# Attention followed by a two-layer feed-forward block: q and k of batches 1 to 7 turned by crossbar DMA instead of TensorE, and another way to set up the bias band

## The chip, the cores and the metric

The kernel runs on one NeuronCore of a Trainium2 chip. Its engines work side by side, each through its own queue of instructions: TensorE (PE: matmuls, and its weight loads, PEld), VectorE (DVE), ScalarE (ACT), GpSimd (POOL) and SyncE (SP). Transfers are issued from the queues of SP and POOL and carried out by 16 shared DMA engines. The metric is the device time of one execution in microseconds (us). The runs of the kernel before took 419.15 us in the median (418.38 to 419.69).

## The reference

Inputs are q, k and v of 8 batches, 8 heads, 576 tokens and 64 numbers a head, a bias table of 32 buckets by 8 heads, and the two weight matrices (512 x 2048 and 2048 x 512). All are float32.

```
scores = scale * q @ k^T                      # 576 x 576 for each batch and head
bias   = bias_table[bucket(|i - j|)]          # depends only on |i - j|; from 128 on one bucket
attn   = exp(scores + bias - max) ; attn /= sum(attn)
x      = (attn @ v), heads side by side       # 4608 x 512
h      = x @ w_in ; g = max(0.01 h, h) ; out = g @ w_out
```

The output is 4608 x 512, float32.

## The kernel before

**Items.** The work on attention goes over 32 pairs of heads: item n is batch n // 4 and pair n % 4. The loop at line 410 runs over n, and each round does the scores and exps of pair n, the product with V of pair n - 1, and the transposition of q and k of pair n + 1. In the gaps it places pieces of the feed-forward block (`moe(1)`, lines 428 to 457), four matmuls of 512 columns each, at most eight in a round, alternately of the first and of the second layer. A tile of 512 tokens of the first layer can start once the batches that it needs are finished, so there is none before round 4 ends. What is left is done at the end (`moe_rest`).

**q and k.** GpSimd loads them by cast DMA (`load_qk`, L106) in bfloat16, 96 partitions with six consecutive tokens each. `pair_rows` (L219) copies the two heads of a pair side by side on VectorE. `transpose_q` and `transpose_k` (L227, L238) turn six blocks of 96 x 128 on TensorE into a PSUM tile of the pool `ps_m`, which has three buffers and also serves the feed-forward block; then VectorE copies them to SBUF and puts the tokens in their order (L234, L245). The last 64 keys of each head are copied once more behind the others (L249).

**Scores to output.** `qk_mm` (L252) makes scores with keys on the partitions, in six parts a pair (L259, L265, L268, L269); ScalarE takes the exp (L279 to L286); `band` (L294) multiplies the parts near the diagonal by exp(bias - bias of the last bucket), which is 1 further away. `av` (L310) multiplies with V and a column of ones, and VectorE divides (L326, L327). `x_transposes` (L330) turns the result for the feed-forward block. Its output goes out by SP (L364) from a pool of four buffers.

**The bias band.** The exponentials of the table, 8 heads on 8 partitions, are spread on VectorE into a row of 512 numbers a head (L147 to L165). SP writes the rows (8 KB) to DRAM and reads them back in two transfers to `hk`, each partition one element further than the last (L166 to L173). This gives the band mirrored, and `make_band` (L175) turns it round into `eb`, with a copy for the last 64 keys in `eb4`: pair 0 on VectorE, pairs 1 to 3 on GpSimd. In round 0 the band products of pair 0 are put off to the end of the round (L287 to L292), so that VectorE prepares pair 1 before.

**Order.** The program gives the order on every engine in the order of its lines: L68 lists PE, ACT, DVE, POOL and SP. On GpSimd the loads for batch 1, the weights and V of batch 1 (L415 to L419) therefore stand behind the three `make_band` calls. Later batches are loaded in round p = 1 of the batch before (L420). VectorE's buffer memsets (L187 to L195) stand behind the work on the bias rows.

Of the kernel before, what the change touches and what calls it, by code (L numbers as in the profile page):

```python
# [10 lines left out]
FP32 = mybir.dt.float32  # L11
BF16 = mybir.dt.bfloat16

AF = mybir.ActivationFunctionType
ALU = mybir.AluOpType
# [22 lines left out]
def kernel(  # L38
# [26 lines left out]
    n_cc = DM // P  # L65
    BAND = 128

    ctx.enter_context(tc.manual_schedule(engines={ET.PE, ET.Activation, ET.DVE, ET.Pool, ET.SP}))  # L68

    per = ctx.enter_context(tc.tile_pool(name="per", bufs=1))  # L70
    qt_pool = ctx.enter_context(tc.tile_pool(name="qt", bufs=2))
    pr_pool = ctx.enter_context(tc.tile_pool(name="pr", bufs=4))
    op_pool = ctx.enter_context(tc.tile_pool(name="op", bufs=2))
    rc_pool = ctx.enter_context(tc.tile_pool(name="rc", bufs=4))
    gt_pool = ctx.enter_context(tc.tile_pool(name="gt", bufs=2))
# [3 lines left out]
    ps_m_pool = ctx.enter_context(tc.tile_pool(name="ps_m", bufs=3, space=bass.MemoryType.PSUM))  # L79

    ident = per.tile([P, P], BF16, name="ident")
    warm = per.tile([P, 1], FP32, name="warm")
    nc.vector.memset(warm, 0.0)
    nc.scalar.activation(warm, warm, AF.Exp)

    xT = [per.tile([P, NT], BF16, name=f"xT{p}") for p in range(n_pairs)]
    w_in_sb = per.tile([P, n_cc, DF], BF16, name="w_in_sb")
# [44 lines left out]
                in_=v[b, h0 + e : h1 : 2, NJ * P : S, :].rearrange("h s d -> s h d"),  # L132
            )

    tabT = per.tile([H, NB], FP32, name="tabT")
    with nc.allow_non_contiguous_dma(reason="a table of 256 numbers"):
        nc.sync.dma_start(out=tabT, in_=bias_table.rearrange("u h -> h u"))
    load_qk(0, 0, 2)
    make_identity(nc, ident)

    e8 = per.tile([H, NB], BF16, name="e8")
    UW = 4 * P
    BW = 3 * P
    ub = per.tile([H, UW], BF16, name="ub")
    nc.vector.memset(ub, 1.0)  # L147
    negc = per.tile([H, 1], FP32, name="negc")
    nc.vector.tensor_scalar(negc, tabT[:, NB - 1 : NB], -1.0, None, op0=ALU.mult)
    nc.scalar.activation(e8, tabT, AF.Exp, bias=negc[:, 0:1], scale=1.0)  # L150
    C0 = 2 * P - 1
    small = NB // 2
    nc.vector.tensor_copy(out=ub[:, C0 : C0 + small], in_=e8[:, 0:small])
    for u, lo, hi in bucket_runs(NB, BAND, S):
        if lo >= small:
            nc.vector.tensor_copy(
                out=ub[:, C0 + lo : C0 + hi + 1],
                in_=e8[:, u : u + 1].to_broadcast([H, hi - lo + 1]),
            )
    row = ub[:, :]  # L160
    nc.vector.tensor_copy(
        out=ub[:, C0 - BAND + 1 : C0],
        in_=bass.AP(tensor=row.tensor, offset=row.offset + C0 + BAND - 1,
                    ap=[list(row.ap[0]), [-1, BAND - 1]]),
    )  # L165
    udr = nc.dram_tensor("u_row", [H, UW], BF16, kind="Internal")  # L166
    hk = per.tile([P, H, BW], BF16, name="hk")
    nc.sync.dma_start(out=udr.ap(), in_=ub)
    for h0, h1 in ((0, 2), (2, H)):
        nc.sync.dma_start(  # L170
            out=hk[:, h0:h1, :],
            in_=bass.AP(tensor=udr, offset=h0 * UW, ap=[[1, P], [UW, h1 - h0], [1, BW]]),
        )  # L173

    def make_band(eng, p):  # L175
        t = hk[:, 2 * p : 2 * p + 2, :]
        eng.tensor_copy(
            out=eb[:, 2 * p : 2 * p + 2, :],
            in_=bass.AP(tensor=t.tensor, offset=t.offset + BW - 1,
                        ap=[list(t.ap[0]), [BW, 2], [-1, BW]]),  # L180
        )
        for e in range(2):
            r = slice(e * SL, (e + 1) * SL)
            eng.tensor_copy(out=eb4[r, p, :], in_=eb[r, 2 * p + e, e * SL : e * SL + P + SL])

    load_qk(0, 2, H)
    for i in range(NBUF):  # L187
        nc.vector.memset(v4[i], 0.0)
        for e in range(2):
# [2 lines left out]
    for i in range(2):  # L192
        nc.vector.memset(kts_[i][:, S : S + P], 0.0)
        nc.vector.memset(at_[i][:, ATW : ATW + SL], 1.0)
        nc.vector.memset(at4_[i][:, S : S + SL], 1.0)  # L195
    load_v(0, 0, 2, True)
    load_v(0, 2, H, False)
    for j in range(1, n_pairs):
        make_band(nc.gpsimd, j)

    def load_w_in(half):
        o = slice(half * (DF // 2), (half + 1) * (DF // 2))
        for c in range(n_cc):
            nc.gpsimd.dma_start(out=w_in_sb[:, c, o], in_=moe_w_in[c * P : (c + 1) * P, o])

    def load_w_out():
        for g in range(n_fc // 4):
            nc.gpsimd.dma_start(
                out=w_out_sb[:, 4 * g : 4 * g + 4, :],
                in_=moe_w_out[g * 512 : (g + 1) * 512, :].rearrange("(f p) e -> p f e", p=P),  # L210
            )
# [2 lines left out]
    items = [(b, p) for b in range(B) for p in range(n_pairs)]  # L214
    qts, kts, ops_ = {}, {}, {}

    prs = {}

    def pair_rows(n, which):  # L219
        src = {"q": qn, "k": kn}[which]  # L220
        b, p = items[n]
        t = pr_pool.tile([RQ, NC, 2 * D], BF16, name="pr")
        nc.vector.tensor_copy(out=t.rearrange("r c (e d) -> r c e d", e=2),  # L223
                              in_=src[b % NBUF][0:RQ, 2 * p : 2 * p + 2, :, :].rearrange("r e c d -> r c e d"))
        prs[n, which] = t

    def transpose_q(n):  # L227
        qs = prs.pop((n, "q"))
        ps = ps_m_pool.tile([P, 8 * P], BF16, name="ps_tq", tag="m")
        for c in range(NC):  # L230
            nc.tensor.transpose(ps[:, c * RQ : (c + 1) * RQ], in_=qs[0:RQ, c, :],  # L231
                                identity=ident[0:RQ, 0:RQ])
        qt = qt_pool.tile([P, S], BF16, name="qt")
        nc.vector.tensor_copy(out=qt.rearrange("p (r c) -> p r c", c=NC),  # L234
                              in_=ps[:, 0:S].rearrange("p (c r) -> p r c", c=NC))
        qts[n] = qt

    def transpose_k(n):  # L238
        ks = prs.pop((n, "k"))
        ps = ps_m_pool.tile([P, 8 * P], BF16, name="ps_tk", tag="m")  # L240
        for c in range(NC):
            nc.tensor.transpose(ps[:, c * RQ : (c + 1) * RQ], in_=ks[0:RQ, c, :],  # L242
                                identity=ident[0:RQ, 0:RQ])
        kt = kts_[n % 2]
        nc.vector.tensor_copy(out=kt[:, 0:S].rearrange("p (r c) -> p r c", c=NC),  # L245
                              in_=ps[:, 0:S].rearrange("p (c r) -> p r c", c=NC))
        for e in range(2):
            r = slice(e * D, (e + 1) * D)
            nc.vector.tensor_copy(out=kt[r, S + e * SL : S + (e + 1) * SL], in_=kt[r, NJ * P : S])  # L249
        kts[n] = kt  # L250

    def qk_mm(n, u):  # L252

# [21 lines left out]
    def exp_band(n, u, ps):  # L275
        b, p = items[n]
        at, at4 = at_view(n), at4_[n % 2]
        if u < NJ:
            nc.scalar.activation(at[:, :, u, 0:512], ps, AF.Exp, scale=scale)  # L279
        elif u == NJ:  # L280
            nc.scalar.activation(  # L281
                at[:, :, :, 512:S],
                ps[:, :, 0 : NJ * SL].rearrange("p e (c i) -> p e c i", i=SL),
                AF.Exp, scale=scale)
        else:
            nc.scalar.activation(at4[:, 0:S], ps.rearrange("p e i -> p (e i)")[:, 0:S], AF.Exp, scale=scale)  # L286
        if n > 0:  # L287
            band(n, u)
        elif u == NJ + 1:
            make_band(nc.vector, 0)  # L290
            for j in range(NJ + 2):
                band(n, j)  # L292

    def band(n, u):  # L294
        b, p = items[n]
# [106 lines left out]
            while made["ready"] < n_tt and (made["ready"] + 1) * TT <= (b + 1) * S:  # L402
                made["ready"] += 1

    pair_rows(0, "q")
    pair_rows(0, "k")
    transpose_q(0)
    transpose_k(0)
    N = len(items)
    for n in range(N + 1):  # L410
        live = n < N
        if live:
            b, p = items[n]
            if n == 0:
                load_qk(1, 0, H)  # L415
                load_w_in(0)
                load_w_in(1)
                load_v(1, 0, H, False)
                load_w_out()  # L419
            elif p == 1 and 0 < b < B - 1:  # L420
                load_qk(b + 1, 0, H)
                load_v(b + 1, 0, H, False)
            if n + 1 < N:
                pair_rows(n + 1, "q")
                pair_rows(n + 1, "k")
            ps_a, ps_b = qk_mm(n, 0), qk_mm(n, 1)
            exp_band(n, 0, ps_a)
        moe(1)
        if live:
            exp_band(n, 1, ps_b)  # L430
        if n > 0:
            av(n - 1, 0)
        if n + 1 < N:
            transpose_q(n + 1)
        moe(1)
        if live:
            ps_a, ps_b = qk_mm(n, 2), qk_mm(n, 3)
            exp_band(n, 2, ps_a)
        moe(1)
        if live:  # L440
            exp_band(n, 3, ps_b)
        if n > 0:
            av(n - 1, 1)
        if n + 1 < N:
            transpose_k(n + 1)
        moe(1)
        if live:
            ps_a, ps_b = qk_mm(n, 4), qk_mm(n, 5)
            exp_band(n, 4, ps_a)
        moe(1)  # L450
        if n > 0:
            x_transposes(n - 1)
            finished(n - 1)
        moe(1)
        if live:
            exp_band(n, 5, ps_b)
        moe(2)
# [31 lines left out]
```

The softmax here doesn't subtract the row's maximum and nothing guards it: scores larger than these inputs give would overflow.

## Time and profile before

| | us |
|---|---|
| median of the runs | 419.15 |
| the profiled execution | 419.69 |
| its span, from first to last instruction | 417.9 |
| TensorE busy in the span | 394.9 |
| ScalarE busy | 247.0 |
| VectorE busy | 226.7 |
| GpSimd busy | 67.9 |

A line of the stages gives a stretch of the span, then for each engine its busy time and the number of its instructions, the granted clock of TensorE, the share of the DMA engines and what they moved. A line of the chain of waits gives the start, the length and what the time went to: an engine's work on a tile with its line, or a transfer. A line of the groups gives line, engine, operation, tile, shapes and count, then busy time and the mean of one in ns, then the idle time before it and what ended it. PEld lines are weight loads, which overlap matmuls. "issue" is time in which nothing that the profile shows was waited for. Numbers behind a tile's name tell buffers apart.

### The profile page before, as it was taken

Reading aid. Unit: us, or ns where it says so; the run is one execution under the profiler, and the core shown is the slowest. Engines: PE = TensorE matmul, PEld = TensorE weight load, DVE = VectorE, ACT = ScalarE, POOL = GpSimd, SP = SyncE. Lnnn points to the kernel's source line nnn. Section 1 sums busy time; section 2 is a strip of 40 time slices with the busy share of each in tenths; the row PEclk is TensorE's granted clock in tenths of the full one; section 3 lists DMA queues with packets and bytes.
Section 4 is the critical chain, followed back from the end, with each engine's and each line's share of the span. In section 5 each row is a group of like instructions: output and inputs, shape, how many; then the busy total and the mean of one; then the engine's idle time right before and its main releaser. Section 6 shows DMA issues by size and latency. Waiting matters only on the chain.

```text
span 417.9 us, 9069 instructions
## 1 busy us (share of the span) xinstructions
PE 394.9 (94%) x3872; PEld 203.8 (49%) x3872; DVE 226.7 (54%) x585; ACT 247.0 (59%) x339; POOL 67.9 (16%) x97
## 2 busy tenths in 40 slices
PE   1897699999999999999999999999999999999996
PEld 1365365455555555445554455555555454444442
DVE  6789667765666655655566666655666431010111
ACT  1768477866666676666666666667666633333310
POOL 8474631301022100410041004000000000000000
PEclk9999999999999999999999999999999999999999
DMA  8969999458027710944091706300000001010112
GB/s 115 131 99 202 183 204 166 36 33 140 27 37 71 123 44 27 83 75 91 25 83 30 137 27 39 46 25 27 27 27 27 27 27 50 25 52 25 52 50 76
DMA packets 60096, 29.16 MB, mean 70 GB/s; under 512 B 39056, under 2 KB 54424, under 8 KB 60056
## 3 DMA queue, kind: packets, MB, share of 16 engines
q0 software_dynamic: 53536, 18.36, 40.5%
q1 hardware_dynamic: 6520, 10.24, 6.8%
q8 instruction: 30, 0.49, 0.5%
q14 instruction: 10, 0.08, 0.1%
HBM read 37.49 MB, written 9.45 MB: 112 GB/s over the span
## 4 chain that ended last, share of the span: by engine, by line
PE 82%; DMA 8%; ACT 3%; POOL 2%; DVE 2%; issue 1%; SPq 0%
PE ps_o L321 7%; PE ps_s L259 6%; DMA w_in_sb<-in_moe_w_in_dram 3%; DMA vn_104<-in_v_dram 2%; PE ps_s L268 2%; PE ps_o L323 2%; DMA hk<-u_row 2%; PE ps_tx L335 2%; PE ps_tq L231 1%; PE ps_tk L242 1%; PE ps_s L265 1%; ACT at_109 L279 1%; DMA u_row<-ub 1%; PE pm_5795 L358 1%; PE pm_4291 L358 1%; PE pm_4115 L358 1%
## 5 line engine op out<-in xcount | busy, mean ns | idle before, releaser
L347 PEld LDWEIGHTS <-w_in_sb 128*128 128x128 bf16 x576 | 50.0, 98 | 73.3 <-issue 22.6
L279 ACT ACTIVATE at_109<-ps_s 128x1024 bf16<-128x1024 f32 x64 | 64.4, 1021 | 22.7 <-PE ps_s L259 22.6
L358 PEld LDWEIGHTS <-gt 128*128 128x128 bf16 x576 | 52.5, 98 | 51.4 <-issue 0.4
L279 ACT ACTIVATE at_110<-ps_s 128x1024 bf16<-128x1024 f32 x64 | 64.8, 1021 | 20.1 <-PE ps_s L259 20.1
L308 DVE TENSOR_TENSOR at_110<-at_110,eb 128x512 bf16<-128x512 bf16 (+1 forms) x64 | 32.5, 510 | 44.4 <-ACT at_110 L279 39.7
L308 DVE TENSOR_TENSOR at_109<-at_109,eb 128x512 bf16<-128x512 bf16 (+1 forms) x64 | 32.0, 505 | 39.0 <-ACT at_109 L279 36.6
L321 PEld LDWEIGHTS <-at_109 128*128 128x128 bf16 x640 | 29.3, 101 | 13.2 <-DVE opair L327 3.9
L327 DVE TENSOR_TENSOR opair<-ps_o,rcp 128x320 bf16<-128x320 f32 x64 | 31.5, 491 | 2.2
L321 PEld LDWEIGHTS <-at_110 128*128 128x128 bf16 x640 | 27.8, 99 | 10.0 <-DVE opair L327 3.0
L125 POOL DMA_DIRECT2D vn_104<-in_v_dram x16 | 14.2, 898 | 70.0 <-PE ps_o L323 39.9
L234 DVE COPY qt<-ps_tq 128x576 bf16<-128x576 bf16 x32 | 23.9, 747 | 0.5 <-PE ps_tq L231 0.5
L259 PE MATMUL ps_s<-qt,kt_107 64*128 64x512 bf16 x128 | 21.4, 403 | 2.1 <-DVE kt_107 L245 1.2
L125 POOL DMA_DIRECT2D vn_103<-in_v_dram x16 | 13.9, 881 | 55.5 <-PE ps_o L323 53.0
L231 PE MATMUL ps_tq<-ident,pr 96*128 96x96 bf16 x192 | 14.2, 213 | 7.9 <-DVE pr L223 7.8
L259 PE MATMUL ps_s<-qt,kt_108 64*128 64x512 bf16 x128 | 20.9, 398 | 0.7 <-ACT at_110 L279 0.3
L326 DVE RECIPROCAL rcp<-ps_o 128x5 f32<-128x5 f32 x64 | 12.2, 190 | 14.6 <-PE ps_o L323 14.6
L321 PE MATMUL ps_o<-vn_103,at_109 128*128 128x65 bf16 x320 | 16.1, 200 | 2.4 <-DVE opair L327 2.1
L321 PE MATMUL ps_o<-vn_104,at_109 128*128 128x65 bf16 x320 | 15.4, 197 | 2.2 <-DMA vn_104<-in_v_dram 2.2
L323 PEld LDWEIGHTS <-at_0_111 128*128 128x128 bf16 x160 | 16.1, 100 | 1.1 <-issue 0.8
L321 PE MATMUL ps_o<-vn_103,at_110 128*128 128x65 bf16 x320 | 15.1, 197 | 1.5 <-DVE opair L327 1.5
L281 ACT ACTIVATE at_110<-ps_s 128x512 bf16<-128x512 f32 x16 | 9.6, 598 | 10.9 <-PE ps_s L265 10.9
L323 PEld LDWEIGHTS <-at_1_112 128*128 128x128 bf16 x160 | 15.8, 98 | 0.2 <-DVE at_1_112 L308 0.2
(873 smaller groups left out, 814.7 us busy)
## 6 DMA issues: line engine op xcount, KB each, us to landing
out_dram<-y SPq DMA_DIRECT2D x36, 256.0 KB, 2.0
qn_100<-in_q_dram POOLq DMA_DIRECT2D x4, 576.0 KB, 6.1
kn_102<-in_k_dram POOLq DMA_DIRECT2D x4, 576.0 KB, 8.2
w_in_sb<-in_moe_w_in_dram POOLq DMA_DIRECT2D x8, 256.0 KB, 11.6
vn_104<-in_v_dram POOLq DMA_DIRECT2D x16, 128.0 KB, 4.9
w_out_sb<-in_moe_w_out_dram POOLq DMA_DIRECT2D x4, 512.0 KB, 10.0
qn_99<-in_q_dram POOLq DMA_DIRECT2D x3, 576.0 KB, 6.1
kn_101<-in_k_dram POOLq DMA_DIRECT2D x3, 576.0 KB, 9.4
```

Source lines behind the costliest of these rows:

```text
L125: nc.gpsimd.dma_start(out=vn[i][:, c, h0:h1, 0:D], in_=v[b, h0:h1, c * P : (c + 1) * P, :].rearrange("h s d -> s h d"),)
L231: nc.tensor.transpose(ps[:, c * RQ : (c + 1) * RQ], in_=qs[0:RQ, c, :], identity=ident[0:RQ, 0:RQ])
L234: nc.vector.tensor_copy(out=qt.rearrange("p (r c) -> p r c", c=NC), in_=ps[:, 0:S].rearrange("p (c r) -> p r c", c=NC))
L259: nc.tensor.matmul(ps[:, e, :], lhsT=kt[r, u * P : (u + 1) * P], rhs=qt[r, 0:512], start=True, stop=True)
L279: nc.scalar.activation(at[:, :, u, 0:512], ps, AF.Exp, scale=scale)
L308: nc.vector.tensor_tensor(out=o, in0=o, in1=m, op=ALU.mult)
L321: nc.tensor.matmul(ps[:, ic, :], lhsT=at[:, o : o + P], rhs=vn[i][:, c, 2 * p + e, :], start=(c == 0), stop=False)
L323: nc.tensor.matmul(ps[:, ic, :], lhsT=at4[:, ic * P : (ic + 1) * P], rhs=v4[i][:, p, e, :], start=False, stop=True)
L326: nc.vector.reciprocal(rcp, ps[:, :, D : D + 1])
L327: nc.vector.tensor_tensor(out=opair[:, :, e * D : (e + 1) * D], in0=ps[:, :, 0:D], in1=rcp.to_broadcast([P, NJ + 1, D]), op=ALU.mult)
L347: nc.tensor.matmul(pm, lhsT=w_in_sb[:, c, f * P : (f + 1) * P], rhs=xT[c][:, t0 : t0 + TT], start=(c == 0), stop=(c == n_cc - 1))
L358: nc.tensor.matmul(pm, lhsT=gt[:, f, ts * P : (ts + 1) * P], rhs=w_out_sb[:, f, :], start=(f == 0), stop=(f == n_fc - 1))
```

## The change

The change has four parts.

1. q and k of batches 1 to 7 are no longer turned by TensorE. `pair_rows` copies q and k of a pair into one tile of 96 x 1536, in round n for pair n + 2, and SP issues one crossbar transpose of it into a tile of 128 x 12 x 96 in SBUF (`turn_by_dma`). `transpose_q` and `transpose_k` stand where they stood; for these batches they hold only VectorE's copy to token order, now out of SBUF. Batch 0 is turned by TensorE as before. The pools of the two tiles have three buffers each.
2. The bias rows are made on all 128 partitions, from a table read to all of them, and written to DRAM 128 times (1 MB). The band is read back unmirrored, straight into `eb` and `eb4`, by four transfers. `make_band` and the put-off of pair 0's band products are gone, and so is ScalarE's first activation on an empty column.
3. The buffer memsets now stand ahead of the work on the rows. GpSimd's loads of batch 0 stand ahead of it too; q and k of later batches are loaded one round earlier (p = 0). The first-layer weights come in four transfers instead of eight, and all weights ahead of V of batch 1.
4. The order on POOL and SP is no longer fixed by the program's lines; the scheduler of the framework sets it.

```diff
-    ctx.enter_context(tc.manual_schedule(engines={ET.PE, ET.Activation, ET.DVE, ET.Pool, ET.SP}))
+    ctx.enter_context(tc.manual_schedule(engines={ET.PE, ET.Activation, ET.DVE}))
...
-    pr_pool = ctx.enter_context(tc.tile_pool(name="pr", bufs=4))
+    pr_pool = ctx.enter_context(tc.tile_pool(name="pr", bufs=3))
+    tu_pool = ctx.enter_context(tc.tile_pool(name="tu", bufs=3))
...
-    warm = per.tile([P, 1], FP32, name="warm")
-    nc.vector.memset(warm, 0.0)
-    nc.scalar.activation(warm, warm, AF.Exp)
+    make_identity(nc, ident)
...
-    ub = per.tile([H, UW], BF16, name="ub")
-    nc.vector.memset(ub, 1.0)
...
-    nc.sync.dma_start(out=udr.ap(), in_=ub)
-    for h0, h1 in ((0, 2), (2, H)):
-        nc.sync.dma_start(
-            out=hk[:, h0:h1, :],
-            in_=bass.AP(tensor=udr, offset=h0 * UW, ap=[[1, P], [UW, h1 - h0], [1, BW]]),
-        )
-
-    def make_band(eng, p):
...
     for i in range(NBUF):
         nc.vector.memset(v4[i], 0.0)
...
+    load_qk(0, 0, 2)
     load_v(0, 0, 2, True)
+    load_qk(0, 2, H)
     load_v(0, 2, H, False)
-    for j in range(1, n_pairs):
-        make_band(nc.gpsimd, j)
...
+    tab = per.tile([P, NB, H], FP32, name="tab")
+    nc.sync.dma_start(
+        out=tab.rearrange("p u h -> p (u h)"),
+        in_=bass.AP(tensor=bias_table.tensor, offset=bias_table.offset, ap=[[0, P], [1, NB * H]]),
+    )
+    UW = 4 * P
+    ub = per.tile([P, H, UW], BF16, name="ub")
+    nc.vector.memset(ub, 1.0)
+    nc.vector.tensor_tensor(out=tab, in0=tab, in1=tab[:, NB - 1 : NB, :].to_broadcast([P, NB, H]), op=ALU.subtract)
+    e8 = per.tile([P, H, NB], BF16, name="e8")
+    nc.scalar.activation(e8, tab.rearrange("p u h -> p h u"), AF.Exp)
...
+    urows = nc.dram_tensor("u_rows", [P, H, UW], BF16, kind="Internal")
+    for h0, h1 in ((0, 2), (2, H)):
+        nc.sync.dma_start(out=urows.ap()[:, h0:h1, :], in_=ub[:, h0:h1, :])
+    for h0, h1 in ((0, 2), (2, H)):
+        nc.sync.dma_start(
+            out=eb[:, h0:h1, :],
+            in_=bass.AP(tensor=urows, offset=h0 * UW + P - 1, ap=[[H * UW - 1, P], [UW, h1 - h0], [1, 3 * P]]),
+        )
+    for e in range(2):
+        nc.sync.dma_start(
+            out=eb4[e * SL : (e + 1) * SL, :, :],
+            in_=bass.AP(tensor=urows, offset=e * UW + P - 1, ap=[[H * UW - 1, SL], [2 * UW, n_pairs], [1, P + SL]]),
+        )
...
+    def pair_rows(n):
+
+        b, p = items[n]
+        t = prs[n] = pr_pool.tile([RQ, 2, NC, 2 * D], BF16, name="pr")
+        for j, src in enumerate((qn, kn)):
+            nc.vector.tensor_copy(out=t[:, j, :, :].rearrange("r c (e d) -> r c e d", e=2),
+                                  in_=src[b % NBUF][0:RQ, 2 * p : 2 * p + 2, :, :].rearrange("r e c d -> r c e d"))
+
+    def by_dma(n):
+        return items[n][0] > 0
+
+    def turn_by_dma(n):
+        t = turned[n] = tu_pool.tile([P, 2 * NC, RQ], BF16, name="tu")
+        nc.sync.dma_start_transpose(out=t, in_=prs.pop(n).rearrange("r j c d -> r (j c d)"))
+
+    def turned_pair(n, j):
+
+        if by_dma(n):
+            return turned[n][:, j * NC : (j + 1) * NC, :].rearrange("p c r -> p r c")
+        ps = ps_m_pool.tile([P, 8 * P], BF16, name="ps_t", tag="m")
+        for c in range(NC):
+            nc.tensor.transpose(ps[:, c * RQ : (c + 1) * RQ], in_=prs[n][0:RQ, j, c, :],
+                                identity=ident[0:RQ, 0:RQ])
+        return ps[:, 0:S].rearrange("p (c r) -> p r c", c=NC)
+
     def transpose_q(n):
...
+        qt = qts[n] = qt_pool.tile([P, S], BF16, name="qt")
+        nc.vector.tensor_copy(out=qt.rearrange("p (r c) -> p r c", c=NC), in_=turned_pair(n, 0))
...
-        if n > 0:
-            band(n, u)
-        elif u == NJ + 1:
-            make_band(nc.vector, 0)
-            for j in range(NJ + 2):
-                band(n, j)
+        band(n, u)
...
                 load_qk(1, 0, H)
-                load_w_in(0)
-                load_w_in(1)
+                load_weights()
                 load_v(1, 0, H, False)
-                load_w_out()
+            elif p == 0 and 0 < b < B - 1:
+                load_qk(b + 1, 0, H)
             elif p == 1 and 0 < b < B - 1:
-                load_qk(b + 1, 0, H)
                 load_v(b + 1, 0, H, False)
...
+            if n + 1 < N and not by_dma(n + 1):
+                pair_rows(n + 1)
+            if n + 2 < N and by_dma(n + 2):
+                pair_rows(n + 2)
+                turn_by_dma(n + 2)
```

More of the change, by code (lines that the diff above doesn't have):

```diff
@@ L133, in load_v @@
             )
[L135 to L145, printed above, removed]
-    ub = per.tile([H, UW], BF16, name="ub")
-    nc.vector.memset(ub, 1.0)
[L148 to L158, printed above, removed]
-            )
[L160 to L167, printed above, removed]
-    nc.sync.dma_start(out=udr.ap(), in_=ub)
-    for h0, h1 in ((0, 2), (2, H)):
-        nc.sync.dma_start(
-            out=hk[:, h0:h1, :],
-            in_=bass.AP(tensor=udr, offset=h0 * UW, ap=[[1, P], [UW, h1 - h0], [1, BW]]),
-        )
-    def make_band(eng, p):
[L176 to L186, printed above, removed]
     for i in range(NBUF):
@@ L195 @@
         nc.vector.memset(at4_[i][:, S : S + SL], 1.0)
+    load_qk(0, 0, 2)
     load_v(0, 0, 2, True)
+    load_qk(0, 2, H)
     load_v(0, 2, H, False)
-    for j in range(1, n_pairs):
-        make_band(nc.gpsimd, j)
-    def load_w_in(half):
-        o = slice(half * (DF // 2), (half + 1) * (DF // 2))
+    tab = per.tile([P, NB, H], FP32, name="tab")
[3 more added lines that the diff above has]
+    )
@@ new lines @@
+    UW = 4 * P
[4 more added lines that the diff above has]
+    nc.scalar.activation(e8, tab.rearrange("p u h -> p h u"), AF.Exp)
+    C0 = 2 * P - 1
+    small = NB // 2
+    nc.vector.tensor_copy(out=ub[:, :, C0 : C0 + small], in_=e8[:, :, 0:small])
+    for u, lo, hi in bucket_runs(NB, BAND, S):
+        if lo >= small:
+            nc.vector.tensor_copy(
+                out=ub[:, :, C0 + lo : C0 + hi + 1],
+                in_=e8[:, :, u : u + 1].to_broadcast([P, H, hi - lo + 1]),
+            )
@@ new lines @@
+    row = ub[:, :, :]
+    nc.vector.tensor_copy(
+        out=ub[:, :, C0 - BAND + 1 : C0],
+        in_=bass.AP(tensor=row.tensor, offset=row.offset + C0 + BAND - 1,
+                    ap=[list(row.ap[0]), [UW, H], [-1, BAND - 1]]),
+    )
[6 more added lines that the diff above has]
+            in_=bass.AP(tensor=urows, offset=h0 * UW + P - 1, ap=[[H * UW - 1, P], [UW, h1 - h0], [1, 3 * P]]),
+        )
@@ L203, in load_w_in, with load_weights @@
+    for e in range(2):
+        nc.sync.dma_start(
+            out=eb4[e * SL : (e + 1) * SL, :, :],
+            in_=bass.AP(tensor=urows, offset=e * UW + P - 1, ap=[[H * UW - 1, SL], [2 * UW, n_pairs], [1, P + SL]]),
+        )
+    def load_weights():
         for c in range(n_cc):
-            nc.gpsimd.dma_start(out=w_in_sb[:, c, o], in_=moe_w_in[c * P : (c + 1) * P, o])
-    def load_w_out():
+            nc.gpsimd.dma_start(out=w_in_sb[:, c, :], in_=moe_w_in[c * P : (c + 1) * P, :])
         for g in range(n_fc // 4):
@@ L215 @@
     qts, kts, ops_ = {}, {}, {}
-    prs = {}
-    def pair_rows(n, which):
-        src = {"q": qn, "k": kn}[which]
+    prs, turned = {}, {}
+    def pair_rows(n):
         b, p = items[n]
[L222 to L225, printed above, removed]
-    def transpose_q(n):
[L228 to L236, printed above, removed]
@@ L238, in transpose_k @@
-    def transpose_k(n):
[L239 to L246, printed above, removed]
+        t = prs[n] = pr_pool.tile([RQ, 2, NC, 2 * D], BF16, name="pr")
@@ L247, in transpose_k @@
+    def transpose_q(n):
+        qt = qts[n] = qt_pool.tile([P, S], BF16, name="qt")
+        nc.vector.tensor_copy(out=qt.rearrange("p (r c) -> p r c", c=NC), in_=turned_pair(n, 0))
+    def transpose_k(n):
+        kt = kts[n] = kts_[n % 2]
+        nc.vector.tensor_copy(out=kt[:, 0:S].rearrange("p (r c) -> p r c", c=NC), in_=turned_pair(n, 1))
         for e in range(2):
@@ L249, in transpose_k @@
             nc.vector.tensor_copy(out=kt[r, S + e * SL : S + (e + 1) * SL], in_=kt[r, NJ * P : S])
-        kts[n] = kt
     def qk_mm(n, u):
@@ L403, in finished @@
                 made["ready"] += 1
-    pair_rows(0, "q")
-    pair_rows(0, "k")
+    pair_rows(0)
     transpose_q(0)
@@ L415 @@
                 load_qk(1, 0, H)
-                load_w_in(0)
-                load_w_in(1)
+                load_weights()
                 load_v(1, 0, H, False)
-                load_w_out()
+            elif p == 0 and 0 < b < B - 1:
+                load_qk(b + 1, 0, H)
             elif p == 1 and 0 < b < B - 1:
-                load_qk(b + 1, 0, H)
                 load_v(b + 1, 0, H, False)
-            if n + 1 < N:
-                pair_rows(n + 1, "q")
-                pair_rows(n + 1, "k")
+            if n + 1 < N and not by_dma(n + 1):
[3 more added lines that the diff above has]
+                turn_by_dma(n + 2)
             ps_a, ps_b = qk_mm(n, 0), qk_mm(n, 1)
```

## The prediction

> **What bounds the kernel now.** I read the whole-span rows first, then busy time by stage, then the chain of work in two stretches, then the rows of what the change touches. The page, engines and slices:
>
> ```profile
> PE 394.9 (94%) x3872; PEld 203.8 (49%) x3872; DVE 226.7 (54%) x585; ACT 247.0 (59%) x339; POOL 67.9 (16%) x97
> ...
> PE   1897699999999999999999999999999999999996
> ```
>
> Busy time by stage (span of the stage, then busy us and instructions of each engine):
>
> ```profile
> 30.00:40.00 10.00, 8.05 (x129) 4.98 (x129) 9.19 (x26) 8.13 (x11) 4.39 (x6) 1.00 1.16 202
> 40.00:50.00 10.00, 5.84 (x84) 3.42 (x85) 6.46 (x17) 5.80 (x8) 5.03 (x8) 1.00 1.72 182
> ...
> 160.00:200.00 40.00, 40.00 (x433) 20.64 (x432) 24.46 (x61) 26.90 (x37) 6.31 (x8) 1.00 0.51 72
> ```
>
> There are two regimes. From about 80 us PE never rests, while VectorE is 61% and ScalarE 67% busy; before that PE has gaps. The chain in the steady stage is PE work end to end, and the transposes of q and k are links of it:
>
> ```profile
> 163.52 0.26 PE ps_tq L231 x6
> 163.78 0.86 PE pm_2584 L358 x4
> ...
> 166.92 0.26 PE ps_tk L242 x6
> 167.18 0.86 PE pm_2584 L358 x4
> ```
>
> The first score matmuls (L259) of two pairs stand at 161.19 and 172.28, so a pair takes 11.09 us, of which 0.26 + 0.26 = 0.52 us is these transposes. Each matmul row shows 0.2 us (14.2 us for a line in the union), but they are pipelined, and the chain's 0.26 us for six is what PE pays. In the first 50 us the chain is made of transfers:
>
> ```profile
> 4.99 4.93 DMA u_row<-ub
> 9.93 0.40 SPq L170
> 10.34 0.04 issue
> 10.38 7.68 DMA hk<-u_row
> 18.05 0.05 issue
> 18.11 1.08 POOL eb L177
> ...
> 26.11 11.04 DMA w_in_sb<-in_moe_w_in_dram
> ...
> 39.45 9.69 DMA vn_104<-in_v_dram
> ```
>
> So GpSimd makes bands until 24 us, the loads queued behind them start there, and V of batch 1 lands at 49.1. Score matmuls begin at 10.0, 15.1, 24.4, 30.7, 37.2, 45.2, 57.0, 65.5, 74.0 and 83.6 us for pairs 0 to 9, and at 327.5 for the last.
>
> **What the Trainium skill says.** "DMA: Bandwidth & Descriptors", section "DMA Transpose (X-bar)": the plain crossbar transpose can only be issued by Sync or ScalarE; so it stands in SP's queue with the output stores. Its section "Issuing engines are not separate DMA queues": all queues share the 16 DMA engines, so the new transfers and the loads slow each other. The trace agrees: while hk was read beside the loads, 192 KB took 5.2 us and 576 KB 7.7. "VectorE: DVE Perf Modes", section "What auto-detection actually checks": a one-source operation from SBUF to SBUF can use two ports, one from PSUM cannot. The trace agrees: 768 elements SBUF to SBUF take 0.35 us (0.36 mirrored), 576 out of PSUM 0.75 us.
>
> **The change, part by part.**
>
> *PE transposes.* Twelve fewer for each of 28 pairs. Where PE is the bound, iterations 9 to 30 (they prepare pairs 10 to 31): 22 x 0.52 = 11.4 us, and about half of iteration 8, 0.2: -11.6 us. Iterations 3 to 7 are not bound by PE (the chain there alternates between exps and score matmuls), so nothing is counted.
>
> *The copies to token order.* 56 of them go from PSUM to SBUF as source, same 576 elements. 0.75 us if nothing improves, 0.36 if two ports engage; I take 0.4. VectorE has 39% slack in the steady stage, so this is worth nothing there. The pair-row copies stay at 0.35 each, only one pair earlier.
>
> ```profile
> L234 DVE COPY qt<-ps_tq 128x576 bf16<-128x576 bf16 x32 | 23.9, 747 | 0.5 <-PE ps_tq L231 0.5
> ```
>
> *The crossbar transfers.* 28, each 96 rows x 1536 columns x 2 bytes = 295 KB. No row shows one. From below: "DMA: Bandwidth & Descriptors", section "Latency and other measured facts", has 261 GB/s, 1.1 us, and some 2 us to land (the output stores' figure here): about 3. From above: the 1309 ns for 128x128 in "VectorE: DVE Perf Modes", section "The three transpose paths", is eight blocks of 16 rows by 128 columns; 72 blocks at that rate would be 11.8 us. Between them, an estimate from this trace: rows of 256 bytes make 1152 packets, 72 per DMA engine. The software queue below spent 0.405 x 418 x 16 / 53,536 = 51 ns on a packet, the hardware queue 70, so 3.6 to 5 us, and 5 to 7 with landing. I take 6.
>
> ```profile
> q0 software_dynamic: 53536, 18.36, 40.5%
> q1 hardware_dynamic: 6520, 10.24, 6.8%
> ```
>
> Issued some 1 us into iteration n for pair n+2, it is wanted by VectorE's q copy 5.3 us into the next (pair rows at 160.3, q copy at 165.45): 10.6 + 4 = 14 us of cover in the steady stage and about 9 before, and one per 10.6 us as the rate. At 6 us the wait is nothing. If late, the q copy blocks VectorE, and behind it are band products, reciprocals and the k copy, then PE's next scores. On SP nothing else waits but output stores, which have four buffers. That SP's and GpSimd's order is no longer written out can shift a store ahead of a transfer; the cover of 14 us hides one such wait.
>
> *The start.* Removed: the row on 8 partitions, its 8 KB write, two reads into hk, and one plus three make_bands. Added on VectorE ahead of pair 0: the buffer memsets come first (5.01 to 7.43, 2.4 us), then a 4096-element memset (512 took 0.48: 3.8), a subtraction (0.4, nearest row 320 elements at 0.49), a wait for an exp of 256 (0.45), and the row's copies, eight times longer: 0.2, then 15 for 1.2 + 784 x 0.9 ns = 1.9, then the mirror 0.5. Starting at 0.8 the rows are ready at about 10.5 us, against 4.97. ScalarE's dropped warm-up costs nothing if its table still loads at 0.74 while it waits; 1.3 us otherwise. SP then writes 1 MB: 4.9 us as for 8 KB, plus 1 MB at about 200 GB/s (the rate while hk was read), 5: landed at 20.5 (16.7 if the read of two heads waits only for its own 256 KB; near 30 if the write shares badly with the loads). The read of two heads, 192 KB, as hk's: 5.2, so 25.7, against 15.1. The other heads and the two eb4 reads land near 29.
>
> Now bands of pair 0 are no longer put off, so VectorE stands at the first one, and queued behind it are q and k of pair 1. From 25.7 its queue is: two bands 1.0, q 0.75, band 0.55, k with tails 1.1, bands 0.75; then for pair 1 rows 0.7, bands 1.0, normalizing 0.7, q 0.75, band 0.55, normalizing 0.7, k 1.1. With small waits the scores of pair 2 begin some 9 us on, at 34.7 instead of 24.4: +10.3. Pair rows of pair 0, 3.2 us later than before, are under that wait.
>
> Some comes back. GpSimd no longer waits for hk or makes bands, so the loads start near 14 instead of 24 us; 2 MB of new traffic takes most of that, but V of batch 1 (landing near 50) is then ahead of its reader near 54. Iteration 5, 11.8 us before, becomes 8.5 like the next two: -3.4. Iteration 3's two copies save 0.8. The first crossbar transfers share engines with weight loads (72 x (51 + 70) ns = 8.7 us against a cover of 9): I charge 1.0. At pair 9 the sum is 10.3 - 3.4 - 0.8 + 1.0 = +7.1.
>
> *Sum:* 7.1 - 11.6 = -4.5. The profiled execution was 419.69 (span 417.9, 1.8 around it), 0.5 above the median of 419.15; so 415.2 profiled, 414.7 as a median.
>
> **Rivals.**
>
> *The crossbar sets the pace* (slower). The first transfer is issued near 36 us; if each takes t and they follow one another, the last lands at 36 + 28t, 1 us later the last pair can start, and 92 us follow as now (419.7 - 327.5): 129 + 28t. It decides from t = 10.4 us on; at 11.8 the time is 459. For it: the isolated 1309 ns, and writes of a few bytes per partition; against it: the packet estimate and the skill's bandwidths (also 350 to 400 GB/s in "Advanced Engine Details and Errata", section "X-Bar Transpose (TRN2)").
>
> *The start eats the gain.* If the 1 MB lands near 26 instead of 20.5 and V of batch 1 is late again, the delay at pair 9 is 12 and the time about 420. For it: DMA engines are full from 2 to 18 us.
>
> *The start costs little.* If the first read waits for 256 KB alone (-3.8) and packets do not collide (-1.0), 410; if the prologue catches up fully, 406. For it: the 7 us in which the DMA engines idled around 20 us.
>
> **How the numbers follow.** Forecast 0.56 (own range 410 to 418), crossbar pace 0.22, start eats it 0.14, cheap start 0.08. A change of 0.3%, 1.3 us, is about what can be told from none. Faster: 0.53 + 0.08 = 0.61. Same: 0.03 of the forecast's edge and 0.06 of the second rival: 0.09. Slower: 0.22 + 0.08 = 0.30. The range reaches from the cheap start, 406, to a crossbar just past its deciding point, 431; 0.17 of the first rival lies above, 0.02 below.
>
> **What would show it.** Right: no ps_tq or ps_tk matmuls after batch 0; a steady pair of 10.57 us with PE full; crossbar transfers landing within 10 us and no wait of VectorE for them; first band product near 26 us; scores of pair 9 near 91. Wrong: VectorE's q copy waiting on a DMA in every iteration and pairs at the transfer's pace; PE gaps after 90 us; a first band product after 32.

## The result, and the profile after

The changed kernel takes 435.6 us in the median (435.08 to 436.23) beside 418.76 for the kernel before: 1.040 times the time, 95% interval 1.037 to 1.043. The prediction had 414.7 us and a range up to 431. Its profiled execution has a span of 433.6 us, 15.7 more than before.

Engines and slices of the changed kernel, from its page:

```profile
PE 378.8 (87%) x3536; PEld 189.6 (44%) x3536; DVE 223.9 (52%) x581; ACT 246.9 (57%) x338; POOL 60.7 (14%) x84
...
PE   0520836888999999999999999999999999999996
```

TensorE has 336 matmuls fewer and is busy 16 us less, and yet the span grew. The slices show where: the first ten (108 us) are full of holes. The stages say the same (span, then busy us and instructions of PE, PEld, DVE, ACT, POOL, then the granted clock, the share of the DMA engines and GB/s):

```profile
20.00:30.00 10.00, 0.00 (x0) 0.00 (x0) 2.63 (x5) 0.00 (x0) 2.12 (x3) 1.00 1.17 220
...
60.00:70.00 10.00, 3.30 (x36) 2.12 (x38) 4.54 (x14) 1.94 (x2) 0.00 (x0) 0.55 0.84 78
...
160.00:200.00 40.00, 40.00 (x390) 19.66 (x388) 24.48 (x64) 27.75 (x39) 6.34 (x8) 1.00 0.80 96
```

Between 20 and 30 us TensorE does nothing; between 60 and 70 us it is busy for a third, at a granted clock of 0.55. From 110 us on it is full again. The chain of waits in the first 75 us names three transfers:

```profile
11.58 7.77 DMA u_rows<-ub
...
21.23 20.69 DMA eb_102<-u_rows
...
42.03 0.27 DVE at_0_115 L292
...
49.86 15.02 DMA tu<-pr
64.88 0.02 issue
64.90 0.64 DVE qt L232
```

VectorE's own rows of that time say how long it stood (the bracket is the idle time before the instruction, and what ended it):

```profile
27.37 0.89 DVE L292 TENSOR_TENSOR at_113<-at_113,eb 128x512 bf16<-128x512 bf16 x2 [12.42 <-DMA eb<-u_rows]
...
42.03 0.26 DVE L292 TENSOR_TENSOR at_0_115<-at_0_115,eb_102 128x192 bf16<-128x192 bf16 x1 [11.05 <-DMA eb_102<-u_rows]
...
64.90 0.64 DVE L232 COPY qt<-tu 128x576 bf16<-128x576 bf16 x1 [7.57 <-DMA tu<-pr]
```

So there are three waits: for the band's first part, which the prediction had; for its last part (`eb4`); and for the first crossbar transfer. That transfer went out at 49.86 us. Half a microsecond earlier GpSimd had issued the load of q of batch 2, which had waited for VectorE to copy the rows of pair 3, the last that were read from that buffer:

```profile
49.32 0.88 POOL L108 DMA_DIRECT2D qn_103<-in_q_dram  x1 [4.81 <-DVE pr L210]
```

Next in VectorE's order come the rows of pair 4, which let the transfer go. The change itself puts the two together, and later too: at 152.69, 194.97 and 237.26 us a load of q and a transfer leave in the same moment.

The scores of pair 9 begin at 110.60 us, against 83.59 before: 27.0 us late. From there the changed kernel is faster. The chain in its steady stage goes from the product with V straight to the next feed-forward piece, where before 0.26 us of transposes stood between them:

```profile
112.78 0.12 PE ps_o L305 x4
112.94 0.86 PE pm_1301 L342 x4
113.80 0.54 PE ps_s L248 x4
```

Pairs 9 and 10 begin at 110.60 and 121.19: 10.59 us instead of 11.09. The last pair begins at 343.18 instead of 327.50. The lateness has come down to 15.7 us, 11.3 less over 22 rounds, and the 90.4 us that follow are the same in both. The gain was made; the start cost over twice as much.

The transfers themselves (KB of each, then the median us from issue to landing):

```profile
u_rows<-ub SPq DMA_DIRECT2D x1, 768.0 KB, 7.8
eb<-u_rows SPq DMA_DIRECT2D x1, 576.0 KB, 18.5
tu<-pr SPq DMA_TRANSPOSE x28, 4.4
...
eb<-u_rows SPq DMA_DIRECT2D x1, 192.0 KB, 7.8
eb_102<-u_rows SPq DMA_DIRECT2D x2, 96.0 KB, 20.2
```

The reads of the band have the sizes of hk's reads before (5.2 and 7.7 us), and take up to 20 us. The crossbar transfer takes 4.4 us in the median, between 3.3 and 15.0.

### The profile page after: what moved, and what is told of

The parts are those of the page before. It is cut to its first block, busy times and chain, and to the rows that moved or that the text cites. A ratio compares the mean times of both kernels' runs of the same rounds, so it can differ in the third digit from the quotient of the medians.

```text
span 433.6 us, 8439 instructions
## 1 busy us (share of the span) xinstructions
PE 378.8 (87%) x3536; PEld 189.6 (44%) x3536; DVE 223.9 (52%) x581; ACT 246.9 (57%) x338; POOL 60.7 (14%) x84
## 4 chain that ended last, share of the span: by engine, by line
PE 77%; DMA 10%; DVE 6%; ACT 4%; issue 1%; SPq 0%; DVEq 0%; ACTq 0%
PE ps_o L305 7%; PE ps_s L248 6%; DMA eb_102<-u_rows 5%; DMA tu<-pr 3%; PE ps_s L257 2%; PE ps_o L307 2%; DMA u_rows<-ub 2%; PE ps_tx L319 2%; ACT at_113 L268 1%; ACT at_114 L268 1%; PE ps_s L254 1%; ACT gt L333 1%; DVE ub L157 1%; PE pm_5412 L342 1%; DVE at_113 L292 1%
## 5 line engine op out<-in xcount | busy, mean ns | idle before, releaser
L305 PEld LDWEIGHTS <-at_113 128*128 128x128 bf16 x640 | 28.3, 100 | 10.0 <-DVE opair L311 5.0
L305 PEld LDWEIGHTS <-at_114 128*128 128x128 bf16 x640 | 27.7, 99 | 10.2 <-DVE opair L311 5.2
L248 PE MATMUL ps_s<-qt,kt_112 64*128 64x512 bf16 x128 | 20.8, 396 | 12.9 <-DVE kt_112 L236 11.5
L307 PE MATMUL ps_o<-v_0_109,at_0_115 128*128 128x65 bf16 x80 | 13.7, 200 | 10.1 <-DVE at_0_115 L292 10.0
L232 DVE COPY qt<-tu 128x576 bf16<-128x576 bf16 x28 | 18.1, 646 | 7.6 <-DMA tu<-pr 7.6
L319 PE MATMUL ps_tx<-ident,opair 128*128 128x128 bf16 x160 | 14.6, 223 | 8.0 <-DVE opair L311 8.0
L307 PEld LDWEIGHTS <-at_0_115 128*128 128x128 bf16 x160 | 15.9, 99 | 10.4 <-DVE at_0_115 L292 10.4
L129 POOL DMA_DIRECT2D v_1_110<-in_v_dram x8 | 5.1, 642 | 96.2 <-PE ps_o L307 91.4
L319 PEld LDWEIGHTS <-opair 128*128 128x128 bf16 x160 | 11.7, 100 | 15.7 <-DVE opair L311 8.9
L129 POOL DMA_DIRECT2D v_0_109<-in_v_dram x10 | 6.4, 643 | 83.7 <-PE ps_o L307 83.7
L305 PE MATMUL ps_o<-vn_107,at_113 128*128 128x65 bf16 x320 | 15.8, 200 | 0.8 <-DVE opair L311 0.8
L248 PEld LDWEIGHTS <-kt_112 64*128 64x128 bf16 x128 | 4.5, 94 | 27.3 <-issue 14.3
L124 POOL DMA_DIRECT2D vn_108<-in_v_dram x16 | 14.1, 888 | 15.0 <-PE ps_o L307 7.0
## 6 DMA issues: line engine op xcount, KB each, us to landing
kn_106<-in_k_dram POOLq DMA_DIRECT2D x4, 576.0 KB, 15.3
```

Of the source, the lines that this page charges most:

```text
L124: nc.gpsimd.dma_start(out=vn[i][:, c, h0:h1, 0:D], in_=v[b, h0:h1, c * P : (c + 1) * P, :].rearrange("h s d -> s h d"),)
L248: nc.tensor.matmul(ps[:, e, :], lhsT=kt[r, u * P : (u + 1) * P], rhs=qt[r, 0:512], start=True, stop=True)
L305: nc.tensor.matmul(ps[:, ic, :], lhsT=at[:, o : o + P], rhs=vn[i][:, c, 2 * p + e, :], start=(c == 0), stop=False)
L307: nc.tensor.matmul(ps[:, ic, :], lhsT=at4[:, ic * P : (ic + 1) * P], rhs=v4[i][:, p, e, :], start=False, stop=True)
L319: nc.tensor.transpose(ps[:, ic * P : (ic + 1) * P], in_=opair[:, ic, :], identity=ident)
```

## The experiments

The theory after the result: the steady stage gains what was predicted, and the start loses twice, because transfers that VectorE waits for meet loads that GpSimd now issues at once. The rivals: the crossbar itself is the cause, or the size and address pattern of the 1 MB of rows, or the queue order that is no longer written out.

### One part at a time

The bias band, with the change's order of the loads: the changed kernel with every pair turned by TensorE.

```diff
     def by_dma(n):
-        return items[n][0] > 0
+        return items[n][0] > 99
```

> The changed kernel with all q and k turned by TensorE again, so that only its bias band, its load order and its unwritten queue order are left. Theory of the start: it keeps the 11 us that VectorE waits for the last band read, loses the 7.6 us wait for the first crossbar transfer and gives back 11.4 us of transposes: 439 us, between 434 and 443. If the crossbar were the cause of the loss: 417 to 424 us.

Measured: 439.67 us, 1.051 times before (1.048 to 1.054). The two waits for the band are there, 23.9 us together, and its last reads land after 20.4 us. The crossbar is not needed for this part of the loss: pair 9 begins at 102.86 us, 19.3 late, and nothing is won back. Nor is a lower granted clock: it was 1.00 up to 110 us in this run.

The crossbar alone: the kernel before, with the changed kernel's functions for rows, transfer and copies, all else as before.

```diff
-    pr_pool = ctx.enter_context(tc.tile_pool(name="pr", bufs=4))
+    pr_pool = ctx.enter_context(tc.tile_pool(name="pr", bufs=3))
+    tu_pool = ctx.enter_context(tc.tile_pool(name="tu", bufs=3))
...
-            if n + 1 < N:
-                pair_rows(n + 1, "q")
-                pair_rows(n + 1, "k")
+            if n + 1 < N and not by_dma(n + 1):
+                pair_rows(n + 1)
+            if n + 2 < N and by_dma(n + 2):
+                pair_rows(n + 2)
+                turn_by_dma(n + 2)
```

> The kernel before with the crossbar transposes alone (batches 1 to 7, two pairs ahead); bias band, load order and the written order of all queues stay as before. My theory is that the loss of the whole change is made in the start, by band reads and the first crossbar transfers meeting the loads, and that the steady stage gains. Here the band is as fast as before, but loads of batch 1 are issued at 24 us while pair 4's rows are wanted in round 2: VectorE waits some 8 us there, and the first transfer lands 9 to 15 us after its issue. Steady pairs 10.57 us instead of 11.09. 418 us, between 413 and 423. If the crossbar costs the steady stage, pairs stay at 11 us or more and the time is over 425.

Measured: 424.39 us, 1.013 (1.011 to 1.016), slower than expected. Steady pairs take 10.57 us here too (121.07 to 131.64), so the theory's half on the steady stage holds; but the start loses more than I had put down. VectorE waits for transfers three times, and for q and k of the next batch five times:

```profile
DVE qt L247 <- DMA tu<-pr: 9.3, 3, 4.5
...
DVE pr L225 <- DMA kn<-in_k_dram: 7.1, 3, 3.1
...
DVE pr L225 <- DMA qn<-in_q_dram: 5.1, 2, 4.1
```

The columns are us in total, times, and the longest. With the loads in the old order, rows two pairs ahead are wanted before q and k have landed. In three stretches of the start (30 to 39, 47 to 53 and 74 to 80 us) the granted clock was 0.50; what that adds to the loss was not separated.

From batch 2 on: as above, but batch 1 is turned by TensorE too.

```diff
-        return items[n][0] > 0
+        return items[n][0] > 1
```

> As the one above, but batches 0 and 1 are turned by TensorE and the crossbar serves batches 2 to 7 (24 pairs), so that its first transfer is issued near 57 us, when the loads of the weights are nearly through. Theory of the start: nothing of the first 55 us changes, then 22 to 23 rounds at 0.52 us less: 407 us, between 405 and 410. If the crossbar costs more than it frees in the steady stage: 415 us or more.

Measured: 416.66 us, 0.996 (0.993 to 0.998). A miss by 9.7 us: I had overlooked that the first rows of batch 2 are now wanted in round 6, and their load is issued only at 49 us.

```profile
61.70 0.36 DVE L225 COPY pr<-qn 96x768 bf16<-96x768 bf16 x1 [5.27 <-DMA qn<-in_q_dram]
64.90 0.36 DVE L225 COPY pr<-kn 96x768 bf16<-96x768 bf16 x1 [2.85 <-DMA kn<-in_k_dram]
```

Rows, and behind them the bands of pair 6, wait 8.1 us; pair 7 begins at 72.98 instead of 65.51. That the loss was all in the start was tested by the next one.

From pair 10 on: rows of pair 10 are taken in round 8, near 74 us, after that load has landed.

```diff
-        return items[n][0] > 0
+        return n >= 10
```

> The kernel before with crossbar transposes from pair 10 on (22 pairs; pairs 0 to 9 by TensorE), rows and transfer two pairs ahead. In the two runs with the crossbar alone, the time was lost before 80 us: VectorE waited for q and k of the next batch, which the pair rows now want a round earlier, and for transfers that took 13 to 15 us beside the loads. Pair 10's rows come near 74 us, when q and k of batch 2 have landed and the weights are through. If that is all, the start stays as before and rounds 9 to 30 take 0.52 us less each: 407.5 us, between 405 and 410. If some of the loss is in the steady stage: 413 us or more.

Measured: 408.17 us, 0.973 (0.971 to 0.976). That is the whole predicted gain of the steady stage with the old start, and faster than both kernels. The first transfer, at 74 us, landed after 4.9 us. The three that were issued 0.3 us behind the load of q of a later batch, and 0.5 ahead of that of k (near 125, 167 and 209 us), took 12.7 to 15.2. All others whose landing the trace shows took 3.3 to 7.0, among them one that went out 0.7 us ahead of such a load (82.11 us: 6.2). In this stage even the long ones nearly hide under the cover of 14 us: VectorE waited 0.4 us in all.

```profile
DMA to landing us min/median/max: 3.3/5.0/15.2
```

### What makes the start slow

In the kernel before, GpSimd waits for hk in its first band copy, and the loads of batch 1 and the weights stand behind it. The share of the DMA engines between 18 and 26 us of the kernel before, in tenths of 40 slices:

```profile
DMA  1000000000000000000200000000000000000399
```

They are idle. While hk was read (9.9 to 18.1 us) GpSimd issued only the last of batch 0's V, until 14.3 us, and from 17 us on the engines ran dry. The changed kernel has no such wait: there GpSimd issues q and k of batch 1, both weights and V of batch 1 between 11.9 and 45 us, around the band's reads at 19.4 to 21.2. So one copy of one element per partition was put back, which reads `eb4` on GpSimd ahead of the weights (GpSimd's order is written out, so that it stays there; that line and the tile's are left out here):

```diff
                 load_qk(1, 0, H)
+                nc.gpsimd.tensor_copy(out=gate, in_=eb4[:, 0, 0:1])
                 load_weights()
```

> The changed kernel, with GpSimd's order written out and one element-wide copy on GpSimd that reads the band (eb4) ahead of the weight loads, so that weights and V of batch 1 are issued only when the band has landed. If the loads slow the band reads: the last one takes 8 to 10 us instead of 20 and lands near 30 us, the wait of 11 us goes, weights come later and meet the first crossbar transfer again: 424 us, between 419 and 430. If the size or the address pattern of the 1 MB in DRAM is what makes the reads slow: they still take 18 to 20 us, the weights come after 42 us, and the time is over 436 us.

Measured: 424.85 us, 1.015 (1.013 to 1.018), 10.8 us less than the changed kernel; the wait of 11.05 is gone. The same reads of the same 1 MB:

```profile
eb<-u_rows SPq DMA_DIRECT2D x1, 576.0 KB, 8.5
...
eb<-u_rows SPq DMA_DIRECT2D x1, 192.0 KB, 6.1
eb<-u_rows SPq DMA_DIRECT2D x2, 96.0 KB, 8.0
```

18.5 us became 8.5, and 20.2 became 8.0. The loads that were held back, weights and V of batch 1, made the reads slow; size and pattern did not. From the issue of the first read to the landing of the last, all DMA together moved 1.5 MB in the kernel before (180 GB/s for 8.15 us), 4.9 MB in the changed kernel (218 for 22.6 us) and 1.9 MB here (200 for 9.5 us). The engines were full for most of that time in each of the three; what differs is how much was queued beside the reads. What did not go is the wait for crossbar transfers, 9.8 us in three rounds, since the weights and V of batch 1 now come later and meet the first two of them.

The changed kernel as it is, with crossbar transposes from pair 10 on (the edit shown above), takes the other wait away:

> The changed kernel as it is, but with crossbar transposes from pair 10 on. It splits the loss of the start: without the wait of 7.6 us for the first transfer, the 11 us wait for the last band read stays, and all of the gain of the steady stage: 428 us, between 425 and 431. If the early transfers cost nothing beyond what the band reads cost: 434 us or more.

Measured: 428.27 us, 1.022 (1.020 to 1.024), 7.3 less than the changed kernel.

Both together:

> The changed kernel with both waits of the start taken away: weight loads held until the band has landed, and crossbar transposes from pair 10 on. If the two waits (11.0 and 7.6 us) and the later first band product are all that went wrong: 435.6 - 10.8 - 7.5 = 417.3 us, between 414 and 420, and what is left over 408.2 us is the lateness of the first band product. If the start has another cost: 422 us or more.

Measured: 418.98 us, 1.000 (0.998 to 1.002): as fast as before, 1.7 us over the sum of the two edits. What is left over 408.17 is 10.8 us. In its trace VectorE still waits 10.6 us for the first part of the band; pair 2 begins at 34.97 us, 10.6 late, and pair 9 at 94.42, 10.8 late. The 3.4 us that the prediction had for iteration 5 do not come here: with the weights held, V of batch 1 lands only at 59.4 us, and that iteration takes 13.05 us, where the changed kernel has 8.48. That the first part of the band is what remains is argued from the trace and was not tried alone.

The queue order alone, all five engines listed again in the changed kernel:

```diff
-    ctx.enter_context(tc.manual_schedule(engines={ET.PE, ET.Activation, ET.DVE}))
+    ctx.enter_context(tc.manual_schedule(engines={ET.PE, ET.Activation, ET.DVE, ET.Pool, ET.SP}))
```

> The changed kernel with the order of GpSimd's and SP's queues written out by the program's lines again. If the unwritten order has no part in the loss: 435.6 us within 2 us. If it put a load or a store where it hurt, above all in the start: 430 us or less.

Measured: 436.16 us, 1.041 (1.039 to 1.044). The queue order has no part in it that shows. What the order of the loads in part 3 of the change does by itself was not tried.

### The room of the crossbar

On the kernel with crossbar transposes from pair 10 on, every transfer was issued three times, two of them into tiles that nothing reads (two buffers, in the pool `tx_pool`):

```diff
+        for _ in range(2):
+            x = tx_pool.tile([P, 2 * NC, RQ], BF16, name="tx")
+            nc.sync.dma_start_transpose(out=x, in_=prs[n].rearrange("r j c d -> r (j c d)"))
```

> The kernel before with crossbar transposes from pair 10 on, each issued three times, two of them into two tiles that nothing reads. If transfers overlap in the queue, three need 6.8 us of the DMA engines in a round of 10.6 us, and the time is 408 us within 3 us. If each waits for the landing of the one before (4 to 5 us alone), three need 12 us a round or more and the time is 430 us or more.

Measured: 408.01 us, 0.974 (0.972 to 0.976), no different from one transfer (408.17). Had each waited for the landing of the one before, it would have been over 430 by the estimate above, so transfers overlap.

With six (`range(5)`, four tiles, two output buffers):

> The same with six transfers for each pair (five into four tiles that nothing reads, and two buffers for the output rows instead of four): 13.5 us of the DMA engines in a round, beside the loads. The prediction's rival should now be seen: rounds of 13.5 us or more, 408 + 22 x 3 = 474 us or more. If transfers overlap better than that, under 430 us.

Measured: 460.98 us in a single execution (span 459.2), between the two forecasts. The waits of VectorE:

```profile
DVE qt L252 <- DMA tu<-pr: 57.5, 13, 13.7
```

The span is 53.9 us over that with one transfer. From pair 9 to the last pair it is 50.9 us, 2.3 a round: 12.9 us for six on average. But this is no even pace. Three rounds, those in which q and k of a later batch are loaded, take 23.0, 25.6 and 23.6 us and hold some 40 of the 50.9; most others take 10.6 as with one transfer. After the last load, 30 transfers took 57.3 us from the first issue to the last landing, 1.9 us each, with the DMA engines full (share 1.01). So here the prediction's first rival is real, but where six transfers meet loads, and not by their own time alone. The landing time in this profile is still 4.4 us in the median, so landing is no measure of what the engines are asked for.

## Why the prediction was wrong, point by point

**PE transposes: right.** 22 rounds at 0.52 us were predicted as 11.4 us, and 11.3 were measured between pair 9 and the last.

**The copies: size wrong, without effect.** I took 0.4 us out of SBUF for the two ports that the Trainium skill has in "VectorE: DVE Perf Modes", section "What auto-detection actually checks". The row shows a small gain only, against 747 out of PSUM:

```profile
L232 DVE COPY qt<-tu 128x576 bf16<-128x576 bf16 x28 | 18.1, 646 | 7.6 <-DMA tu<-pr 7.6
```

646 ns for 576 elements is 1.1 ns an element, where the row copies take 0.35 us for 768, 0.46 ns an element. The measurement decides: a copy whose reads step by 192 bytes does not have the speed of the row copies. Whether the step is the reason, and whether one port or two were at work, no run here shows. VectorE had the slack.

**The crossbar price: right in the steady stage, wrong in the start.** I took 6 us to landing; the median is 4.4, and 3.3 the least. The rival with its deciding point t = 10.4 us let each transfer wait for the one before; they overlap. In the steady stage the hardware queue's share between 160 and 240 us rose from 7.0 to 27.2% with 8288 packets more (kernel from batch 2 on): 0.202 x 80 x 16 = 259 engine-us, 31 ns a packet, and for 1152 packets on 16 engines 2.25 us of the engines, with loads beside. The step that failed is "72 x (51 + 70) ns = 8.7 us against a cover of 9: I charge 1.0". It had the neighbours wrong, and with them the size. The last weights landed at 50.2 us, 0.3 us after the first transfer went out; beside V of batch 1 and q and k of batch 2 it took 15.0 us, not 8.7. Nor was the cover 9 us: VectorE wanted it at 57.3, 7.5 us after its issue. It cost 7.6 us of waiting; beginning with pair 10 gave 7.3.

**The start: the failing step.** The rows were ready at 11.2 us (predicted 10.5), the 1 MB landed at 19.4 (20.5), the first band product ran at 27.4 (25.7), and iteration 5 took 8.5 us as predicted. Then: "the other heads and the two eb4 reads land near 29". They landed at 41.9. I had taken hk's 7.7 us as a figure "beside the loads". In the kernel before, only the end of batch 0's loads ran beside hk, some 0.7 MB (1.5 less the 0.8 of hk), because GpSimd waited for hk itself; the same section frees GpSimd from that wait, and sends 4 MB of weights (in bfloat16) and V of batch 1 into the reads. The prediction counted what the freed queue gained, 3.4 us in iteration 5, and not what its transfers would collide with. VectorE stood 11.05 us there.

The sum nearly closes: 7.1 predicted at pair 9, less the 1.0 that it held for the crossbar, + 11.05 for eb4, + 7.57 for the crossbar transfer, + 1.7 for the later first product = 26.4; 27.0 were measured. The sum has no term for the granted clock, which was 0.50 from 65 to 71 us; whether the rest is due to it was not tried.

**The rivals.** "The start eats the gain" was the right place with another mechanism: it looked for a late write of the 1 MB and a delay of 12 us at pair 9. The write was early, and reads and crossbar made it 27. "The crossbar sets the pace" is false at one and three transfers a pair; at six it is true where loads run beside. Of the signs of being wrong that were named, one came: gaps of TensorE after 90 us, up to 108. A wait of VectorE in every iteration did not. The range missed since all its upper end was reserved for the crossbar; two collisions in the start, together 18.6 us, were priced at 1.0.

## What to carry to other kernels

A transfer's time in a profile belongs to what ran beside it: before using it, count what was queued beside it and what will be queued beside the new one. That the engines are full does not tell the two apart; 1.5 and 4.9 MB in the time of the reads do. A wait that is taken out of a queue of loads sets them free against whatever else moves then; here a copy of one element put back was worth 10.8 us. Work that is moved ahead by a round also wants its inputs a round earlier, and the loads have to be moved with it, or the new path begun only once they have landed: that edit turned 424.4 into 408.2 us, and took away the waits for the loads and those for the transfers beside them.

## What was not expected of the hardware

The crossbar transfer of 295 KB takes 2.25 us of all 16 engines beside the loads of the steady stage, 131 GB/s, and 1.9 us in a row of transfers without loads, 155 GB/s. "Advanced Engine Details and Errata", section "X-Bar Transpose (TRN2)", in the Trainium skill expects 350 to 400 GB/s; no run here comes near. Three such transfers a round cost no time, while one beside weights takes 10 to 15 us to land, against 3.3 at the least. Beside loads of q and k it depends on half a microsecond: in the eight traces with one transfer a pair, the 29 that went out between 0.1 us ahead of the load of q and 0.6 us behind it took 9.9 to 15.3 us, the seven that went out 0.7 us ahead of it 6.2 to 8.0. Why the order counts so much, and what in those loads delays the transfer, was not separated and stays open.
